# S1 in a tile of its own and first of seven products, S2·T2 fourth, and the first sigmoid ahead of the conversions

## The chip, the cores and the metric

The kernel runs on one core of a Trainium2 chip. A core has five engines with an instruction queue each: TensorE (PE in the profile, its weight loads PEld), VectorE (DVE), ScalarE (ACT), GpSimd (POOL, here almost only an issuer of DMAs) and SyncE (SP, an issuer of DMAs alone). The metric is the device time of one execution in microseconds (us). The kernel before took 982.21 us, the median of three runs (981.42 to 986.92).

## The reference

Softmaxes over q and k, a linear attention, and then a gated feed-forward layer, all in float32:

```python
q_s = exp(q - max(q, -1));  q_s = q_s / (sum(q_s, -1) + 1e-9)     # q, k, v: 8 x 8 x 576 x 64
k_s = exp(k - max(k, 2));   k_s = k_s / (sum(k_s, 2) + 1e-9)
kv  = einsum('bhsd,bhse->bhde', k_s, v)
x   = einsum('bhsd,bhde->bhse', q_s, kv)  ->  4608 tokens x 512
out = (sigmoid(x @ w_gate) * (x @ w_val)) @ w_out                 # d_ff = 1536
```

The weights come as float64.

## The kernel before, in words

**Tiles.** The 4608 tokens are cut into 9 token tiles of 512 (`w` = 0 to 8), the 1536 hidden columns into 12 blocks of 128 (`j`), or 6 pairs of blocks (`p`).

**First token tile** (w = 0, lines 1006 to 1043). For each `j`, `g1_0(j)` makes gate and value of one block in plain float32, two PSUM tiles of the pool `ps_gv` (three buffers, tile name `gv`); `g_sig_0` (ACT) and `g_mul_0` (DVE) make `h_0`; `g2_0(j-1)` multiplies with the block of w_out. Around them stands all one-time work, written out by hand in the order in which each engine's queue takes it:
- the float64 weights are narrowed to float32 (`w_low`, `w_top`, `w_join`, and `wo_low`, `wo_top`, `wo_join` for w_out), in passes that alternate between DVE and ACT;
- `split_hi` (ACT) and `split_lo` (DVE) split each pair's weights into a rounded part and a remainder, `wo_hi` and `wo_save` do so with w_out, and POOL's queue stores both to DRAM (`s_dram`, `wo_dram`);
- the side work of token tile 1: `k_max_send` and `k_max_read` send the maxima of k through DRAM on POOL's queue (for batches up to 2), and `qT_split(1, hp)` splits the q part that `x_mm(1, hp)` multiplies. It is called in `beside_first`, ahead of the step's conversions, and puts its DVE subtraction (line 514) right behind ACT's copy (line 513).

**Token tiles 1 to 8** (lines 1054 to 1078). 48 steps, one for each token tile and pair. `g1(w, p)` multiplies 2x2 blocks of weights and tokens in Winograd's way: seven products in place of eight, each of 12 matmuls with 256 moving columns (two halves, two row blocks, and three pairs of rounded part and remainder). The stationary operand is a block of weights: A11, A12 and A22 lie in the pair's own tile `a_w[p]`, the sums S1 to S4 in `s_sb`, which every step loads anew (`s_load`, line 278, POOL's queue: the sum for the next step, right behind this step's product). The moving operand is one of seven token blocks (`c_hl`: B11, T1, T2, B21, T3, B22, T4). They accumulate in three PSUM tiles `y`, `z` and `rr`, in the order A11 in y, S1 in z, S2 in y, A12 in rr, S3 in y, S4 in z, A22 in y. y and z are copied out by ACT between products (lines 673, 675, 678, 683), since each copy is a partial sum that the result needs: y after A11, after S2 and after S3. `h_split` makes the stationary operands of `g2`, the 24 matmuls of 512 columns (line 723) that follow one step later. `side_a` and `side_b` put the softmax of the next token tile beside them.

**What sets the order.** Nothing is reordered (`manual_schedule`): each engine works its queue front to back, as the code is written. A matmul that would write a PSUM tile waits until the copy ahead of it has read it. Weight loads run beside the matmul ahead of them.

**Addresses.** Two padding tiles shift pools against each other. Modulo 512 bytes all stationary operands of the split products (`s_sb`, `a_w`, `h`, `kv_sb`) begin at one place, all moving ones (`c_hl`, `wo_hl`, the ring that holds the split q) 320 bytes further on.

Of the kernel before, what the change touches and what calls it, by code (L numbers as in the profile page):

```python
# [8 lines left out]
F32 = mybir.dt.float32  # L9
F32R = mybir.dt.float32r  # L10
# [4 lines left out]
ALU = mybir.AluOpType  # L15
# [36 lines left out]
def attn_moe(ctx: ExitStack, tc: tile.TileContext, qf, qn, qT, k, kT, v, wg, wv, wo, out):  # L52
# [19 lines left out]
    ps_gv = ctx.enter_context(tc.tile_pool(name="ps_gv", bufs=3, space=bass.MemoryType.PSUM))  # L72
    ps_at = ctx.enter_context(tc.tile_pool(name="ps_at", bufs=1, space=bass.MemoryType.PSUM))

    s_sb = const.tile([P, 4, 2, 2, 2 * P], F32R, name="s_sb")
    x_32 = const.tile([P, NP, T], F32, name="x_32")
    sg = const.tile([P, 4, 2, HT], F32, name="sg")
    kv_sb = const.tile([P, 2, 2, NP, P], F32R, name="kv_sb")
# [173 lines left out]

    def split_of(p):
        f = f_w[p].rearrange("p b n e -> p b (n e)")
        s = s_sb.rearrange("p s h n e -> p s h (n e)")
        a = a_w[p].rearrange("p b h n e -> p b h (n e)")
        return [(a[:, A11:A12 + 1], f[:, 0:2])] + [
            (s[:, i:i + 1], t) for i, t in enumerate(s_32[p])
        ] + [(a[:, A22:A22 + 1], f[:, 3:4])]

    def split_hi(p):
# [5 lines left out]
    def split_lo(p):  # L267
        for o, x in split_of(p):
            nc.vector.tensor_tensor(  # L269
                out=o[:, :, 1], in0=x, in1=o[:, :, 0].bitcast(F32), op=ALU.subtract  # L270
            )
        nc.gpsimd.dma_start(
            out=s_dram[p], in_=s_sb.rearrange("p s h n e -> p (s h n e)").bitcast(F32)
        )

    def s_load(p, i):
        n = 4 * 2 * P
        nc.gpsimd.dma_start(  # L278
            out=s_sb[:, i].rearrange("p h n e -> p (h n e)"),
            in_=s_dram[p][:, i * n:(i + 1) * n].bitcast(F32R),  # L280
        )

# [227 lines left out]
    def qT_split(w, hp):  # L510
        t = qT_sb.pop((w, hp))
        hi, lo = (ring.tile([P, T], F32R, name="ring") for _ in range(2))
        nc.scalar.copy(out=hi, in_=t)
        nc.vector.tensor_tensor(out=lo, in0=t, in1=hi.bitcast(F32), op=ALU.subtract)
        qT_hl[w, hp] = (hi, lo)


    x_ps = {}
# [97 lines left out]
    def g_sig_0(j):  # L616
        h_0[j] = two.tile([P, T], F32, name="h_0", tag="h_lo")
        nc.scalar.activation(h_0[j], gate[j][0], AF.Sigmoid)  # L618
# [26 lines left out]
    def g1(w, p, s_next=None):  # L645

        y, z, rr = (ps_gv.tile([P, 2, HT], F32, name="gv") for _ in range(3))
        a, s = a_w[p], s_sb

        def prod(ps, ws, i, first, last):  # L650
            for n in range(2):
                wh, wl = ws(n)
                for kt in range(2):
                    for lh, x in ((wh, 0), (wh, 1), (wl, 0)):
                        nc.tensor.matmul(  # L655
                            ps[:, n], lhsT=lh(kt), rhs=c_hl[i][:, x, kt],
                            start=(first and n == 0 and kt == 0 and lh is wh and x == 0),
                            stop=(last and n == 1 and kt == 1 and lh is wl),
                            skip_group_check=True,
                        )  # L660

        def wa(i):
            return lambda n: [lambda kt, h=h: a[:, i, h, n, kt * P:(kt + 1) * P] for h in range(2)]

        def wsum(i):
            return lambda n: [lambda kt, h=h: s[:, i, h, n, kt * P:(kt + 1) * P] for h in range(2)]

        def more(i):
            if s_next is not None:
                s_load(s_next, i)  # L670

        prod(y, wa(A11), B11, True, False)
        nc.scalar.copy(out=sg[:, 0], in_=y)  # L673
        prod(z, wsum(S1), T1, True, False)
        nc.scalar.copy(out=sg[:, 2], in_=z)  # L675
        more(S1)
        prod(y, wsum(S2), T2, False, False)
        nc.scalar.copy(out=sg[:, 1], in_=y)  # L678
        more(S2)
        prod(rr, wa(A12), B21, True, True)  # L680
        nc.vector.tensor_tensor(out=sg[:, 0], in0=rr, in1=sg[:, 0], op=ALU.add)  # L681
        prod(y, wsum(S3), T3, False, False)
        nc.scalar.copy(out=sg[:, 3], in_=y)  # L683
        more(S3)
        nc.vector.tensor_tensor(out=sg[:, 3], in0=sg[:, 3], in1=sg[:, 2], op=ALU.add)  # L685
        prod(z, wsum(S4), B22, False, True)
        nc.vector.tensor_tensor(out=sg[:, 1], in0=z, in1=sg[:, 1], op=ALU.add)  # L687
        nc.scalar.activation(sg[:, 0:2, 0], sg[:, 0:2, 0], AF.Sigmoid)  # L688
        more(S4)
        prod(y, wa(A22), T4, False, True)  # L690
        nc.scalar.activation(sg[:, 3, 0], sg[:, 3, 0], AF.Sigmoid)
        nc.scalar.activation(sg[:, 2, 0], y[:, 0], AF.Sigmoid)
        tt = nc.vector.tensor_tensor
        tt(out=sg[:, 0:2, 0], in0=sg[:, 0:2, 0], in1=sg[:, 0:2, 1], op=ALU.mult)  # L694
        tt(out=sg[:, 3, 0], in0=sg[:, 3, 0], in1=sg[:, 3, 1], op=ALU.mult)
        tt(out=sg[:, 2, 0], in0=y[:, 1], in1=sg[:, 2, 0], op=ALU.mult)
# [122 lines left out]
    def beside_first(j):  # L819
        if j == 6:  # L820
            k_done(1)
        if 7 <= j <= 10:
            x_ev(1, j - 7)
        if 6 <= j <= 9:
            qT_split(1, j - 6)

    def after_first(j):
        if j == 0:
            for hp in range(NP):
                k_max(1, hp)  # L830
            k_max_send(1)
            k_max_read(1)
        if j == 1:
            for c in range(NC):
                qn_max(1, c)
        if j == 2:
            for c in range(NC):
                qn_sub(1, c)
        if j == 3:
            for c in range(NC):  # L840
                qn_exp(1, c)
            for hp in range(NP):
                k_sum(1, hp)
            for t in range(5):
                k_sub(1, t)
        if j == 4:
            for t in range(5):
                k_exp(1, t)
            for c in range(NC):
                qn_sum(1, c)  # L850
            for hp in range(NP):
                qf_mul(1, hp)
        if j == 5:
            for t in range(5):
                k_mm(1, t)
        if 6 <= j <= 9:
            x_mm(1, j - 6)
        if 5 <= j <= 8:
            qf_tr(1, j - 5, ps_gv.tile([P, T], F32, name="gv"))
        if j in (2, 5, 7, 9):  # L860
            load_next(1, {2: 1, 5: 2, 7: 3, 9: 4}[j])
        if j == 10:
            c_subs()
            load_next(1, 5, range(2))
            for i in (B11, T1, T2, B21):
                c_split(i)
        if j == 11:
            for t in range(2, 5):
                v_load(2, t)
# [135 lines left out]
    splits = {2: 0, 5: 1, 7: 2, 9: 3, 10: 4, 11: 5}  # L1005
    for j in range(NJ):
        g1_0(j)
        beside_first(j)
        split = splits.get(j)
        if split is not None:  # L1010
# [12 lines left out]
            w_low(j + 3)  # L1023
        if j + 2 < NJ:
            wo_low(j + 2)
        g_sig_0(j)
        if j > 0:
            wo_save(j - 1)
        if j + 3 < NJ:
            load_wo(j + 3)  # L1030
        if j + 5 < NJ - 1:
# [9 lines left out]
        if j == 3:  # L1041
            kv_split(0, lambda sl: kv_0[sl, :, sl])
        after_first(j)

    wo_hi(NJ - 1)
    g_mul_0(NJ - 1)
# [70 lines left out]
```

## Time and profile before

| | |
|---|---|
| median of three runs | 982.21 us |
| the profiled execution | 986.01 us |
| its span (first to last instruction) | 984.2 us |
| PE busy, of the span | 954.0 us, 97% |
| ACT, DVE, POOL busy | 471.4, 613.1, 167.3 us |
| mean granted TensorE clock | 0.985 |
| first product of the 48 steps begins | 181.67 us |
| DMA, mean over the span | 262 GB/s |

How to read the profile. The *groups* give for a line, an engine, an operation and its tiles the count, the busy time, the mean time of one, and the idle time of the engine just before, with what ended it. In the *timeline* a row is `start, length, engine, line, operation, tiles, shapes, count`, with the idle time before it and what ended it in brackets; rows of one kind that follow each other are merged. A matmul's length there is a latency: matmuls overlap, and the pace is the distance from start to start. *Waits* list who waited for whom: microseconds in total, times, the longest. The *chain* follows the last instruction back to what released each step.

### The profile page before, as it was taken

The page shows a single profiled execution, that of the slowest core. Times are in us where ns is not written, and L with a number is a line of the kernel's source. Part 1 is how long each engine was busy: PE and PEld are TensorE (multiplying, and loading weights), DVE is VectorE, ACT ScalarE, POOL GpSimd, SP SyncE. Part 2 cuts the span into 40 slices and gives each one's busy share as a digit, 9 for nine tenths or more (in the row PEclk, how much of TensorE's full clock was granted, in tenths as well). Part 3 has the DMA queues.
Part 4 walks back from the last instruction along what each step waited for, and adds up shares of the span by engine and source line. Part 5 has one row for each costly group of instructions (what it writes and reads, how often), then busy time and mean ns, then how long its engine had stood idle before and what let it go on. Part 6 is the DMA issues. An engine that isn't in the chain of part 4 may idle for free.

```text
span 984.2 us, 15634 instructions
## 1 busy us (share of the span) xinstructions
PE 954.0 (97%) x6062; PEld 824.0 (84%) x6062; DVE 613.1 (62%) x1013; ACT 471.4 (48%) x812; POOL 167.3 (17%) x316
## 2 busy tenths in 40 slices
PE   5899999799999999999999999999999999999998
PEld 5544544599999999999989999899999999999997
DVE  8688778776666566755684667557654655463242
ACT  4589785553436354525362545353434434533222
POOL 0110001221122112111111111121112121212210
PEclk7899999899999999999999999999999999999999
DMA  9987484899699978998899869996998779858662
GB/s 337 330 244 267 165 291 166 302 350 323 203 245 361 306 229 212 374 284 259 180 381 304 261 143 375 332 276 132 374 317 239 216 237 312 248 176 251 199 206 74
DMA packets 93864, 257.78 MB, mean 262 GB/s; under 512 B 15264, under 2 KB 17568, under 8 KB 93024
## 3 DMA queue, kind: packets, MB, share of 16 engines
q0 software_dynamic: 43712, 168.32, 56.9%
q1 hardware_dynamic: 50080, 88.48, 30.6%
q8 instruction: 48, 0.79, 0.4%
q14 instruction: 24, 0.20, 0.1%
HBM read 228.20 MB, written 28.56 MB: 261 GB/s over the span
## 4 chain that ended last, share of the span: by engine, by line
PE 66%; DMA 17%; DVE 7%; ACT 7%; issue 2%; SPq 1%; POOL 0%; DVEq 0%; ACTq 0%; POOLq 0%
PE gv L655 37%; PE acc L723 19%; DMA ring<-k_in 3%; DMA q_m_row<-q_m 3%; PE gv L610 3%; DMA q_b<-q_m_row 3%; DMA kmax_row<-k_max 2%; PE gv L538 2%; DMA ring<-qT_in 1%; PE at L378 1%; PE acc L637 1%; DMA ring<-qn_in 1%; DMA s<-s_sb 1%; DMA wo<-wo_hl 1%; PE at L538 1%
## 5 line engine op out<-in xcount | busy, mean ns | idle before, releaser
L655 PE MATMUL gv<-c_hl,s_sb 128*128 128x256 f32 x2304 | 288.1, 280 | 4.3 <-ACT sg L673 4.2
L655 PEld LDWEIGHTS gv<-c_hl,s_sb 128*128 128x128 f32 x2304 | 276.7, 188 | 6.9 <-ACT sg L673 6.5
L723 PE MATMUL acc<-wo_hl,h 128*128 128x512 f32 x1152 | 272.2, 392 | 0.0
L723 PEld LDWEIGHTS acc<-wo_hl,h 128*128 128x128 f32 x1152 | 213.1, 188 | 44.3
L655 PE MATMUL gv<-c_hl,a_w 128*128 128x256 f32 x1728 | 226.1, 279 | 0.7 <-DVE a_w L269 0.7
L655 PEld LDWEIGHTS gv<-c_hl,a_w 128*128 128x128 f32 x1728 | 214.9, 188 | 5.2 <-issue 1.0
L278 POOL DMA_DIRECT2D s_sb<-s x188 | 100.1, 532 | 321.8 <-PE gv L655 317.5
L681 DVE TENSOR_TENSOR sg<-gv,sg 128x512 f32<-128x512 f32 x48 | 33.2, 691 | 163.0 <-PE gv L655 163.0
L234 POOL DMA_DIRECT2D wo_hl<-wo x96 | 50.9, 531 | 297.6 <-PE acc L723 295.4
L683 ACT COPY sg<-gv 128x512 f32<-128x512 f32 x48 | 28.1, 586 | 106.4 <-PE gv L655 106.4
L610 PE MATMUL gv<-x,f_w 128*128 128x512 f32 x160 | 72.4, 606 | 5.5 <-ACT h L618 5.5
L673 ACT COPY sg<-gv 128x512 f32<-128x512 f32 x48 | 28.0, 583 | 89.8 <-PE gv L655 65.1
L685 DVE TENSOR_TENSOR sg<-sg 128x512 f32<-128x512 f32 x48 | 33.2, 692 | 58.9 <-ACT sg L683 58.9
L610 PEld LDWEIGHTS gv<-x,f_w 128*128 128x128 f32 x160 | 30.5, 194 | 43.7 <-issue 36.0
L706 DVE TENSOR_TENSOR h<-sg,h 128x1024 fp32r<-128x1024 f32 x48 | 58.8, 1226 | 1.6
L688 ACT ACTIVATE sg<-sg 128x512 f32<-128x512 f32 x48 | 30.3, 632 | 55.8 <-DVE sg L687 55.8
L694 DVE TENSOR_TENSOR sg<-sg 128x512 f32<-128x512 f32 x48 | 33.2, 693 | 33.5 <-ACT sg L688 33.5
L637 PE MATMUL acc<-wo_t,h 128*128 128x512 f32 x96 | 45.3, 617 | 5.7 <-DVE h L622 5.6
L678 ACT COPY sg<-gv 128x512 f32<-128x512 f32 x48 | 28.1, 586 | 44.7 <-PE gv L655 44.7
L637 PEld LDWEIGHTS acc<-wo_t,h 128*128 128x128 f32 x96 | 18.8, 199 | 30.0 <-issue 21.7
L675 ACT COPY sg<-gv 128x512 f32<-128x512 f32 x48 | 28.1, 586 | 26.2 <-PE gv L655 26.1
L412 ACT CAST kv_sb<-kmax_b 64x256 fp32r<-64x256 f32 x14 | 5.7, 404 | 67.1 <-DVE kmax_b L388 66.8
(152 smaller groups left out, 1054.8 us busy)
## 6 DMA issues: line engine op xcount, KB each, us to landing
s_sb<-s POOLq DMA_DIRECT2D x188, 512.0 KB, 7.6
wo_hl<-wo POOLq DMA_DIRECT2D x96, 512.0 KB, 6.0
s<-s_sb POOLq DMA_DIRECT2D x6, 2048.0 KB, 7.6
out<-x SPq DMA_DIRECT2D x36, 256.0 KB, 9.6
ring<-k_in SPq DMA_DIRECT2D x28, 256.0 KB, 15.0
ring<-qn_in SPq DMA_DIRECT2D x28, 256.0 KB, 10.3
q_b<-q_m_row SPq DMA_DIRECT2D x56, 128.0 KB, 8.6
ring<-qT_in SPq DMA_DIRECT2D x28, 256.0 KB, 8.9
```

What stands on the lines that cost most here:

```text
L234: nc.gpsimd.dma_start(out=t.rearrange("p h e -> p (h e)"), in_=wo_dram[2 * p + i].bitcast(F32R))
L278: nc.gpsimd.dma_start(out=s_sb[:, i].rearrange("p h n e -> p (h n e)"), in_=s_dram[p][:, i * n:(i + 1) * n].bitcast(F32R),)
L538: nc.tensor.matmul(ps[:, f:t], lhsT=kl if lh else kh, rhs=rh[:, f:t], start=(lh == 0 and rh is qh), stop=(lh == 1),)
L610: nc.tensor.matmul(ps[n], lhsT=w[:, kt // 2, sl], rhs=x_0[:, kt], start=(kt == 0), stop=(kt == NK - 1),)
L637: nc.tensor.matmul(acc[0][m], lhsT=h_0[j][:, m * P:(m + 1) * P], rhs=wo_t[j // 2][:, j % 2], start=(j == 0), stop=(j == NJ - 1),)
L655: nc.tensor.matmul(ps[:, n], lhsT=lh(kt), rhs=c_hl[i][:, x, kt], start=(first and n == 0 and kt == 0 and lh is wh and x == 0), stop=(last ...
L681: nc.vector.tensor_tensor(out=sg[:, 0], in0=rr, in1=sg[:, 0], op=ALU.add)
L685: nc.vector.tensor_tensor(out=sg[:, 3], in0=sg[:, 3], in1=sg[:, 2], op=ALU.add)
L688: nc.scalar.activation(sg[:, 0:2, 0], sg[:, 0:2, 0], AF.Sigmoid)
L694: tt(out=sg[:, 0:2, 0], in0=sg[:, 0:2, 0], in1=sg[:, 0:2, 1], op=ALU.mult)
L706: nc.vector.tensor_tensor(out=lo, in0=sg[:, :, 0], in1=hi.bitcast(F32), op=ALU.subtract)
L723: nc.tensor.matmul(acc[w][m], lhsT=h[lh][:, i, sl], rhs=o[i][:, rh], start=(at == 0 and i == 0 and lh == 0 and rh == 0), stop=(at == NS - ...
```

## The change

Four edits. (1) `s_sb` is cut into `s_234` (S2 to S4) and `s_1` (S1), with padding tiles of 80 and 48 words around `s_1`. S1's stationary operand then begins where the moving ones do, modulo 512 bytes; S2 to S4 and everything else stay where they were. The two padding tiles make 512 bytes together. The store of the sums becomes two DMAs. (2) In `g1` S1·T1 comes first, and S2·T2 behind A12·B21 in place of ahead of it. (3) In the first token tile the sigmoid of block 0 comes ahead of the conversions of that step. (4) `qT_split(1, hp)` leaves its DVE subtraction to `qT_low`, called just ahead of `x_mm(1, hp)`, and `wo_save(j-1)` moves behind `after_first(j)`.

```diff
-    s_sb = const.tile([P, 4, 2, 2, 2 * P], F32R, name="s_sb")
+    s_234 = const.tile([P, 3, 2, 2, 2 * P], F32R, name="s_234")
+    const.tile([P, 80], F32, name="pad_s")
+    s_1 = const.tile([P, 1, 2, 2, 2 * P], F32R, name="s_1")
+    const.tile([P, 48], F32, name="pad_x")
+    def s_at(i):
+        return s_1[:, 0] if i == S1 else s_234[:, i - S2]
...
-        nc.gpsimd.dma_start(
-            out=s_dram[p], in_=s_sb.rearrange("p s h n e -> p (s h n e)").bitcast(F32)
-        )
+        n = 4 * 2 * P
+        for t, i0, i1 in ((s_1, 0, 1), (s_234, 1, 4)):
+            nc.gpsimd.dma_start(
+                out=s_dram[p][:, i0 * n:i1 * n],
+                in_=t.rearrange("p s h n e -> p (s h n e)").bitcast(F32),
+            )
...
         hi, lo = (ring.tile([P, T], F32R, name="ring") for _ in range(2))
         nc.scalar.copy(out=hi, in_=t)
+        qT_hl[w, hp] = (hi, lo)
+        if w >= NF:
+            qT_low(w, hp, t)
+        else:
+            qT_sb[w, hp] = t
+
+    def qT_low(w, hp, t):
+        hi, lo = qT_hl[w, hp]
         nc.vector.tensor_tensor(out=lo, in0=t, in1=hi.bitcast(F32), op=ALU.subtract)
-        qT_hl[w, hp] = (hi, lo)
...
-        prod(y, wa(A11), B11, True, False)
-        nc.scalar.copy(out=sg[:, 0], in_=y)
         prod(z, wsum(S1), T1, True, False)
         nc.scalar.copy(out=sg[:, 2], in_=z)
         more(S1)
+        prod(y, wa(A11), B11, True, False)
+        nc.scalar.copy(out=sg[:, 0], in_=y)
+        prod(rr, wa(A12), B21, True, True)
+        nc.vector.tensor_tensor(out=sg[:, 0], in0=rr, in1=sg[:, 0], op=ALU.add)
         prod(y, wsum(S2), T2, False, False)
         nc.scalar.copy(out=sg[:, 1], in_=y)
         more(S2)
-        prod(rr, wa(A12), B21, True, True)
-        nc.vector.tensor_tensor(out=sg[:, 0], in0=rr, in1=sg[:, 0], op=ALU.add)
         prod(y, wsum(S3), T3, False, False)
...
         if 6 <= j <= 9:
+            qT_low(1, j - 6, qT_sb.pop((1, j - 6)))
             x_mm(1, j - 6)
...
         g1_0(j)
+        if j == 0:
+            g_sig_0(j)
         beside_first(j)
...
-        g_sig_0(j)
         if j > 0:
-            wo_save(j - 1)
+            g_sig_0(j)
...
         after_first(j)
+        if j > 0:
+            wo_save(j - 1)
```

**PE, the seven products of one step** (token tile 1, its sixth step), before. `gv_1975` is y, `gv_1976` z and `gv_1977` rr; behind the arrow stand the token block and the weights:

```order
L655 MATMUL gv_1975<-c_hl_1052,a_w_987 128x256 x12
L655 MATMUL gv_1976<-c_hl_1052,s_sb_100 128x256 x12
L655 MATMUL gv_1975<-c_hl_1057,s_sb_100 128x256 x12
L655 MATMUL gv_1977<-c_hl_1057,a_w_987 128x256 x12
L655 MATMUL gv_1975<-c_hl_1104,s_sb_100 128x256 x12
L655 MATMUL gv_1976<-c_hl_1104,s_sb_100 128x256 x12
L655 MATMUL gv_1975<-c_hl_1109,a_w_987 128x256 x12
```

The same step of the changed kernel, where `gv_1984` is y, `gv_1985` z, `gv_1986` rr, and line 673 is what was line 655:

```order
L673 MATMUL gv_1985<-c_hl_1058,s_1_102 128x256 x12
L673 MATMUL gv_1984<-c_hl_1058,a_w_994 128x256 x12
L673 MATMUL gv_1986<-c_hl_1063,a_w_994 128x256 x12
L673 MATMUL gv_1984<-c_hl_1063,s_234_100 128x256 x12
L673 MATMUL gv_1984<-c_hl_1113,s_234_100 128x256 x12
L673 MATMUL gv_1985<-c_hl_1113,s_234_100 128x256 x12
L673 MATMUL gv_1984<-c_hl_1118,a_w_994 128x256 x12
```

Before, no two neighbours write the same PSUM tile. Now the fourth and the fifth (S2 and S3) both write y. With the semaphores that each waits for, the third to the fifth product of the changed kernel read:

```order
L673 MATMUL gv_1986<-c_hl_1063,a_w_994 128x256 [waits Activation_49]
L673 MATMUL gv_1986<-c_hl_1063,a_w_994 128x256 x11
L673 MATMUL gv_1984<-c_hl_1063,s_234_100 128x256 [waits DMASW7_49,Activation_49]
L673 MATMUL gv_1984<-c_hl_1063,s_234_100 128x256 x11
L673 MATMUL gv_1984<-c_hl_1113,s_234_100 128x256 [waits DMASW0_49,Activation_49]
L673 MATMUL gv_1984<-c_hl_1113,s_234_100 128x256 x11
```

The count that the first matmul of the fifth product waits for on ACT's semaphore is that of the copy of y behind the fourth (line 698 of the changed kernel, line 678 before).

**DVE, step j = 9 of the first token tile**, before, from its first row on. `ring<-gv,ring` is the remainder of the split q, `wo_hl` that of w_out (`wo_save`), `a_w` the first row of `split_lo`:

```order
L514 TENSOR_TENSOR ring<-gv,ring 128x512
L169 SCALAR_TENSOR_TENSOR f_last<-f_last,sg 128x2x256 x2
L169 SCALAR_TENSOR_TENSOR wo_t<-wo_t,wo_raw 128x512
L622 TENSOR_TENSOR h_873<-gv,h_873 128x512
L140 TENSOR_SCALAR wo_raw<-wo_raw 128x512
L153 SCALAR_TENSOR_TENSOR wo_raw<-wo_raw 128x512
L222 TENSOR_TENSOR wo_hl<-wo_t,wo_hl 128x512
L269 TENSOR_TENSOR a_w<-f_w,a_w 128x2x512
```

The end of that step in the changed kernel, from the last row of `w_sums(4)` on:

```order
L254 TENSOR_TENSOR s_957<-f_w,s_955 128x512
L533 TENSOR_TENSOR ring<-gv,ring 128x512
L317 TENSOR_REDUCE k_max<-kt_109 128x1
L318 TENSOR_SCALAR k_neg<-k_max 128x1
L317 TENSOR_REDUCE k_max<-kt_110 128x1
L318 TENSOR_SCALAR k_neg<-k_max 128x1
L230 TENSOR_TENSOR wo_hl<-wo_t,wo_hl 128x512
```

The remainder of the split q has gone from the step's first row to a place behind `split_lo` and `w_sums`, and that of w_out from ahead of `split_lo` to behind the maxima of k.

More of the change, by code (lines that the diff above doesn't have):

```diff
@@ L254, in split_of @@
         f = f_w[p].rearrange("p b n e -> p b (n e)")
-        s = s_sb.rearrange("p s h n e -> p s h (n e)")
+        s = [s_at(i).rearrange("p h n e -> p h (n e)").unsqueeze(1) for i in range(4)]
         a = a_w[p].rearrange("p b h n e -> p b h (n e)")
         return [(a[:, A11:A12 + 1], f[:, 0:2])] + [
-            (s[:, i:i + 1], t) for i, t in enumerate(s_32[p])
+            (s[i], t) for i, t in enumerate(s_32[p])
         ] + [(a[:, A22:A22 + 1], f[:, 3:4])]
@@ L278, in s_load @@
         nc.gpsimd.dma_start(
-            out=s_sb[:, i].rearrange("p h n e -> p (h n e)"),
+            out=s_at(i).rearrange("p h n e -> p (h n e)"),
             in_=s_dram[p][:, i * n:(i + 1) * n].bitcast(F32R),
@@ L647, in g1 @@
         y, z, rr = (ps_gv.tile([P, 2, HT], F32, name="gv") for _ in range(3))
-        a, s = a_w[p], s_sb
+        a = a_w[p]
         def prod(ps, ws, i, first, last):
@@ L665, in wsum @@
         def wsum(i):
-            return lambda n: [lambda kt, h=h: s[:, i, h, n, kt * P:(kt + 1) * P] for h in range(2)]
+            return lambda n: [lambda kt, h=h: s_at(i)[:, h, n, kt * P:(kt + 1) * P] for h in range(2)]
         def more(i):
```

## The prediction

> **What bounds the kernel now.** I read the page first: busy time, the chain that ended last, the costliest groups.
>
> ```profile
> PE 954.0 (97%) x6062; PEld 824.0 (84%) x6062; DVE 613.1 (62%) x1013; ACT 471.4 (48%) x812; POOL 167.3 (17%) x316
> PE 66%; DMA 17%; DVE 7%; ACT 7%; issue 2%; SPq 1%; POOL 0%; DVEq 0%; ACTq 0%; POOLq 0%
> L655 PE MATMUL gv<-c_hl,s_sb 128*128 128x256 f32 x2304 | 288.1, 280 | 4.3 <-ACT sg L673 4.2
> L723 PE MATMUL acc<-wo_hl,h 128*128 128x512 f32 x1152 | 272.2, 392 | 0.0
> L655 PE MATMUL gv<-c_hl,a_w 128*128 128x256 f32 x1728 | 226.1, 279 | 0.7 <-DVE a_w L269 0.7
> ```
>
> PE is busy for 97% of the span, and its three costliest groups, the products of the 48 steps and the second multiplication, make 786 of 954 us with hardly any idle time ahead of them. Next I asked who waits in the 48 steps.
>
> ```profile
> PEld gv L655 <- ACT sg L673: 6.5, 11, 0.8
> ```
>
> From 206 us on this is the only wait of PE's weight loads that the view lists, and its matmuls wait for nothing else either: 6.5 us in 11 places, all for the copy of y behind A11. No wait for a DMA appears. So a stall of PE that is added in the steps is added to the time in full, and only these 6.5 us are there to be won back. PE's other waits lie in the first token tile.
>
> **The new wait behind S2.** S2 and S3 now follow each other on y, and S3's first matmul waits for ACT's copy of S2's result. Before, a product on another tile stood between. The timeline has each piece of the new wait, in two steps that lie beside each other:
>
> ```profile
> 301.21 1.52 PE L655 MATMUL gv<-c_hl,a_w 128*128 128x256 f32 x12
> 301.41 0.58 ACT L678 COPY sg<-gv 128x512 f32<-128x512 f32 x1 [0.77 <-PE gv L655]
> ...
> 312.14 1.52 PE L655 MATMUL gv<-c_hl,a_w 128*128 128x256 f32 x12
> ...
> 313.50 1.52 PE L655 MATMUL gv<-c_hl,s_sb 128*128 128x256 f32 x12
> ...
> 314.97 0.56 ACT L673 COPY sg<-gv 128x512 f32<-128x512 f32 x1
> ...
> 315.58 1.68 PE L655 MATMUL gv<-c_hl,s_sb 128*128 128x256 f32 x12 [0.55 <-ACT sg L673]
> ...
> 317.10 1.57 PE L655 MATMUL gv<-c_hl,a_w 128*128 128x256 f32 x12
> ```
>
> ```profile
> L678 ACT COPY sg<-gv x48: 585/587/589, 187.5 to 963.9; 128x512 f32<-128x512 f32 x48
> ```
>
> The copy at 301.41 starts 0.20 us behind the first matmul of the next product (301.21), thus some 0.31 behind the last matmul of its own, one pace of 0.11 earlier. It takes 0.587 (585 to 589 ns in all 48 steps). At 315.53 (314.97 + 0.56) a copy ends for which PE waits, and PE goes on at 315.58, 0.05 later. Unhindered, the next matmul would have come after 0.12. The product that starts out of a wait takes 1.52 from its start to the next one (315.58 to 317.10) where the following ones of that step take 1.41 (1.57 is that plus the last one's latency, as 1.52 is to 1.36 at 312.14): 0.11 more. Together 0.31 + 0.587 + 0.05 - 0.12 + 0.11 = 0.94 us, in each of 48 steps: **+45.1 us**. ACT stands idle ahead of that copy (0.77 us at 301.41), so it can't come earlier; were it late, the wait would be longer. Behind the waiting matmul stand S3, S4, A22 and the 24 matmuls of line 723, and behind these the whole rest: nothing on PE can go around it.
>
> **The old wait goes.** S2 now comes two products behind the start of A11, as before, but S1's copy and A11's have one product more until ACT must have caught up with its backlog. In the step above, S2 starts 2.08 us behind S1 (313.50 to 315.58) in place of 1.36. In the new order S2 would be due at 312.14 + 3 x 1.36 = 316.22; ACT, free at 314.97, has done two copies of 0.587 by 316.14, in time. With the 0.11 behind each of 11 waits, the 6.5 us make 7.7; some 0.1 may stay in two or three steps: **-7.5 us**, between -4 and -8.
>
> The reload of S1 (`s_sb<-s`, issued behind its product) stays a whole step ahead of its use, and that of S2, one product later, is needed one product later.
>
> **S1's own rate, and the two paces.** Steps without any wait differ:
>
> ```profile
> 348.70 1.52 PE L655 MATMUL gv<-c_hl,a_w 128*128 128x256 f32 x12
> ...
> 358.22 5.66 PE L723 MATMUL acc<-wo_hl,h 128*128 128x512 f32 x24
> ...
> 397.74 1.57 PE L655 MATMUL gv<-c_hl,a_w 128*128 128x256 f32 x12
> ...
> 407.63 2.68 PE L723 MATMUL acc<-wo_hl,h 128*128 128x512 f32 x11
> ```
>
> The same 84 matmuls take 9.52 us in one and 9.89 in the other, 113.3 and 117.7 ns each, with the same addresses modulo 512. Counted by these distances, 9 of 48 steps run at the fast pace throughout; the first and the last:
>
> ```profile
> 232.76 1.52 PE L655 MATMUL gv<-c_hl,a_w 128*128 128x256 f32 x12
> ...
> 242.28 1.99 PE L723 MATMUL acc<-wo_hl,h 128*128 128x512 f32 x8
> ```
>
> ```profile
> 753.00 1.52 PE L655 MATMUL gv<-c_hl,a_w 128*128 128x256 f32 x12
> ...
> 762.52 1.76 PE L723 MATMUL acc<-wo_hl,h 128*128 128x512 f32 x7
> ```
>
> So the pace depends on how a step is entered, not on addresses alone. Were all steps fast, the other 39 would give up to 39 x 0.37 = 14 us (13, as some are fast in part). Were all slow, it would cost 3 to 4. After a wait the step above went on slowly (1.41 a product behind 315.58, 1.36 ahead of it), which costs the three products behind the new wait little, since most are slow already: **+1 us**.
>
> What S1's 576 matmuls take with both operands at one remainder, no split product shows. The nearest rows:
>
> ```profile
> 322.75 1.95 PE L378 MATMUL at<-v,ring 128*128 128x128 f32 x16
> ...
> 324.53 3.04 PE L378 MATMUL at<-f_last,ring 128*128 128x128 f32 x24
> ```
>
> ```profile
> 666.37 2.69 PE L538 MATMUL gv<-ring,kv_sb 128*128 128x384 f32 x18
> 668.89 1.03 PE L538 MATMUL at<-ring,kv_sb 128*128 128x384 f32 x6
> ```
>
> ```profile
> 32.50 3.17 PE L561 MATMUL acc<-q,f_last 128*128 128x512 f32 x7
> ...
> 35.51 10.46 PE L610 MATMUL gv<-x,f_w 128*128 128x512 f32 x24
> ```
>
> From below: matmuls with half the columns still take 111 ns (1.78 us for 16), so a pace under 111 is not to be had: 576 x (111 - 117) = -3.5 us. From above: the products of line 538 take 140 ns for 256 columns on average (2.52 us for 18): 576 x 23 = +13. In plain float32 line 561, whose operands do share a remainder, takes 0.43 us a pass (3.01 for 7), and line 610, whose don't, takes the same. I take **0**, by this last and nearest pair, and keep both ends. [...]
>
> **The clock.** A wait of PE can cost clock besides:
>
> ```profile
> 104.00:109.00 5.00, 3.67 (x5) 1.61 (x6) 4.56 (x12) 4.53 (x7) 0.00 (x0) 0.66 0.99 419
> ...
> 312.00:316.00 4.00, 3.45 (x29) 3.21 (x28) 2.94 (x7) 4.00 (x9) 1.07 (x2) 1.00 1.11 405
> ```
>
> In the window with the wait of 0.55 us the granted clock stays at 1.00, while around the 2.01 us of waiting ahead of 105.33 (quoted below) it is 0.66. The new 0.84 us is near the first; I take 0. [...]
>
> **The first token tile.** At its start the sigmoid goes ahead:
>
> ```profile
> 49.41 3.70 PE L610 MATMUL gv<-x,f_w 128*128 128x512 f32 x8 [3.44 <-ACT h L618]
> ...
> 69.18 0.62 ACT L218 CAST wo_hl<-wo_t 128x512 fp32r<-128x512 f32 x1 [4.05 <-DMA wo<-wo_hl]
> ```
>
> ```profile
> 105.33 8.83 PE L610 MATMUL gv<-x,f_w 128*128 128x512 f32 x16 [2.01 <-ACT h L618]
> ```
>
> PE's 3.44 us at 49.41 go, but PE waits for ACT again at 105.33, and ACT's work up to there hangs on the DMA that landed at 69.18, which the edit doesn't touch. I cost it at **0**: the 3.44 us turn up as a longer wait at 105.33. At the end of the tile it is otherwise:
>
> ```profile
> 143.23 0.69 DVE L514 TENSOR_TENSOR ring<-gv,ring 128x512 fp32r<-128x512 f32 x1 [2.79 <-ACT ring L513]
> ```
>
> ```profile
> 156.71 0.76 POOL L319 DMA_DIRECT2D kmax_row<-k_max  x1 [4.22 <-DVE k_neg L307]
> 167.65 0.55 POOL L323 DMA_DIRECT2D kmax_b<-kmax_row  x1 [10.17 <-DMA kmax_row<-k_max]
> ```
>
> ```profile
> 178.05 2.17 ACT L265 CAST s_sb<-s 128x512 fp32r<-128x512 f32 x4 [4.26 <-DMA s<-s_sb]
> ```
>
> ```profile
> 176.55 5.68 PE L637 MATMUL acc<-wo_t,h 128*128 128x512 f32 x8 [5.61 <-DVE h L622]
> ```
>
> The last of these waits is PE's 5.61 us; ACT's at 178.05 hands on to the first product at 181.67. Both end a chain: maxima of k on DVE, sent at 156.71, read at 167.65, and only then the stores of POOL's queue, whose landing frees the sums at 178.05. DVE's 2.79 us of idling at 143.23 lie ahead of the maxima and go; `wo_save`, as large as the row at 143.23 (0.69), moves behind them. So the chain starts 2.79 + 0.69 = 3.5 us earlier: **-3.5 us**, between 0 (if a DMA then lands no earlier) and -5.6 (PE's wait). What is late next is ACT's `split_hi`. The six stores more cost POOL 0.55 us each in idle time; `wo_save` is past `split_lo`'s stores on POOL, and its buffers are wanted again only two steps on.
>
> **The sum**, against the profiled execution's 986.0 us: 986.0 + 45.1 - 7.5 + 1 + 0 - 3.5 + 0 = 1021.1 us, 35.1 more. The profiled execution is 3.8 us above the median of 982.2, which I put down to the paces, so the forecast for the median is **1017.3 us**.
>
> **Rivals.**
> - *All steps fast* (S1 at the front sets the pace). For it: the pace is set at a step's entry. Against: the new wait comes behind it and may set it anew. 13 + 1 us less: 1003.
> - *S1 itself slow.* Up to +13: 1030. Only the rows of line 538 speak for it.
> - *The change doesn't stall*: the copy is hidden. Without the 45.1: 972. Against it stands the order, with S3 behind S2 on one tile and its wait.
> - *The pace itself falls* to 107 ns by S1's new place and order: 4032 x (117 - 107) = 40 us less, 977, faster than before. It decides from 117 - 34/4032 = 109 ns on; below that the kernel is faster. Against it: 111 ns for half the columns.
> - *The clock halves* for some 3.4 us behind each new wait, as around 105.33: 48 x 1.7 = 82 us more, 1099. Against it: 1.00 at 312.
>
> **Chances.** Forecast 0.63, all fast 0.15, S1 slow 0.15, clock 0.03, no stall 0.02, lower pace 0.02. The forecast's own range is 1011 to 1024 (the bounds of the old wait and the first tile); with the first two rivals, 1003 to 1030, and outside stay 0.07 and the far ends. Faster by over 0.5% (about 5 us, what a measurement can tell from no change) comes from the two small cases: 0.04. Within 0.5%: 0.01. Slower: 0.95.
>
> **What would show it.** Right: PE's L673 waits for ACT's L698 48 times, some 0.8 us each by the matmuls' idle time; A11's copy (L694) no longer ends a wait; the first product begins near 178. Wrong: no such wait, or a pace of S1's product far from 113 to 118 ns (12 of them 1.36 to 1.41 us), or products behind the wait that are all fast, or a first product later than 181.67.

## The result: 4% slower, and the profile after

| | before | changed | ratio, 95% interval |
|---|---|---|---|
| runs beside the prediction | 981.82 us (4 runs) | 1021.94 us (2 runs) | 1.0399 [1.0331, 1.0468] |
| repeated, label e1_after | 983.66 us (23 runs) | 1020.04 us (4 runs) | 1.0357 [1.0325, 1.0390] |

The ratios lie near those of the mean times (1021.94 to 982.69 in the first row), not of the medians.

In two other runs of the changed kernel, the profiled one among them, TensorE ran at under a fifth of its pace (5474 us; in the profiled one 679 ns on the mean from matmul to matmul in the products, where e1_after has some 117); they are left out, and the profile shown here is that of e1_after, which is the same kernel (1020.5 us, span 1018.4).

From its page, the engines' busy time and the groups that answer to those of before:

```profile
PE 963.3 (95%) x6062; PEld 826.3 (81%) x6062; DVE 612.8 (60%) x1013; ACT 471.1 (46%) x812; POOL 170.5 (17%) x322
...
L673 PE MATMUL gv<-c_hl,s 128*128 128x256 f32 x2304 | 300.4, 282 | 32.4 <-ACT sg L698 32.4
...
L741 PE MATMUL acc<-wo_hl,h 128*128 128x512 f32 x1152 | 272.6, 392 | 0.0
...
L673 PE MATMUL gv<-c_hl,a_w 128*128 128x256 f32 x1728 | 216.7, 278 | 2.6 <-ACT h L636 2.6
```

PE's work is hardly more than before, but ahead of the products with the sums now stand 32.4 us of idle time, where there were 4.3. The waits of PE and of its weight loads in the steps:

```profile
PEld gv L673 <- ACT sg L698: 42.0, 48, 0.9
...
PE gv L673 <- ACT sg L698: 32.4, 48, 0.7
```

48 waits, one a step, all for ACT's copy of y behind S2. Who waited for the copy behind A11 (line 694), which was PE's only wait in the steps before:

```profile
who waited for it (us, times):
  DVE sg L696: 32.0, 8
  POOL wo L233: 2.7, 1
```

PE is not in that list any more. One step in the timeline (PE, and ACT's copy behind S2):

```profile
334.89 1.60 PE L673 MATMUL gv<-c_hl,s 128*128 128x256 f32 x12
336.33 2.99 PE L673 MATMUL gv<-c_hl,a_w 128*128 128x256 f32 x24
339.16 1.57 PE L673 MATMUL gv<-c_hl,s 128*128 128x256 f32 x12
341.41 3.09 PE L673 MATMUL gv<-c_hl,s 128*128 128x256 f32 x24 [0.68 <-ACT sg L698]
344.34 1.57 PE L673 MATMUL gv<-c_hl,a_w 128*128 128x256 f32 x12
...
340.77 0.58 ACT L698 COPY sg<-gv 128x512 f32<-128x512 f32 x1 [2.24 <-PE gv L673]
```

S2 takes 2.25 us from its start to S3's (339.16 to 341.41) in place of 1.41, and S3 and S4 together 2.93 in place of 2.82: 0.84 + 0.11 = 0.95 us. The copy begins 0.31 behind S2's last matmul (340.46, one pace ahead of 340.57), lasts 0.58, and PE goes on 0.06 behind its end.

To put sums to this, the distances from start to start of all matmuls are taken from the trace, from the third step's first matmul to the program's last (46 steps). A distance of over 205 ns within the products counts as a wait, less 116 ns:

| third step to the end | before | changed |
|---|---|---|
| third step begins | 211.78 us | 207.65 us |
| from there to the last matmul | 768.36 us | 805.96 us |
| waits and the slow matmul behind each | 8.0 us | 43.4 us |
| mean of the other distances in the products | 116.66 ns | 117.13 ns |
| mean distance in line 723 / 741 | 229.72 ns | 229.97 ns |

Of the 37.6 us that the 46 steps lost, 35.4 are waits; the other 2 are pace (0.47 ns on 3726 matmuls are 1.75 us, 0.25 ns on 1082 are 0.27).

### The profile page after: what moved, and what is told of

Its sections match the earlier page's. It is cut to its first block, busy times and chain, and to the rows that moved or that the text cites. A ratio compares the mean times of both kernels' runs of the same rounds, so it can differ in the third digit from the quotient of the medians.

```text
span 5472.1 us, 15649 instructions
## 1 busy us (share of the span) xinstructions
PE 5430.4 (99%) x6062; PEld 4374.7 (80%) x6062; DVE 617.2 (11%) x1013; ACT 478.4 (9%) x812; POOL 169.9 (3%) x322
## 4 chain that ended last, share of the span: by engine, by line
PE 99%; ACT 1%; issue 0%; DVE 0%; POOL 0%; POOLq 0%
PE gv L673 49%; PE acc L741 28%; PE gv L628 9%; PE acc L655 5%; PE at L389 3%; PE gv L556 2%; PE at L556 1%; PE gv L944 1%; ACT sg L698 1%; PE acc L376 0%; PE acc L579 0%; PE gv L511 0%; PE acc L969 0%; PE acc L955 0%; PE at L511 0%
## 5 line engine op out<-in xcount | busy, mean ns | idle before, releaser
L673 PEld LDWEIGHTS gv<-c_hl,s 128*128 128x128 f32 x2304 | 1556.8, 939 | 109.4 <-ACT sg L698 69.0
L673 PE MATMUL gv<-c_hl,s 128*128 128x256 f32 x2304 | 1593.0, 1036 | 32.4 <-ACT sg L698 32.4
L741 PE MATMUL acc<-wo_hl,h 128*128 128x512 f32 x1152 | 1541.5, 1694 | 0.0
L741 PEld LDWEIGHTS acc<-wo_hl,h 128*128 128x128 f32 x1152 | 1033.4, 909 | 436.5 <-issue 421.1
L673 PE MATMUL gv<-c_hl,a_w 128*128 128x256 f32 x1728 | 1179.7, 1034 | 0.0
L673 PEld LDWEIGHTS gv<-c_hl,a_w 128*128 128x128 f32 x1728 | 1172.5, 948 | 0.0
L628 PE MATMUL gv<-x,f_w 128*128 128x512 f32 x160 | 426.3, 3020 | 0.0
L628 PEld LDWEIGHTS gv<-x,f_w 128*128 128x128 f32 x160 | 144.7, 910 | 264.0 <-issue 262.1
L655 PE MATMUL acc<-wo_t,h 128*128 128x512 f32 x96 | 258.4, 3035 | 0.0
L389 PE MATMUL at<-f_last,ring 128*128 128x128 f32 (+1 forms) x160 | 111.7, 1052 | 0.0
```

What stands on the lines that cost most here:

```text
L389: nc.tensor.matmul(kvps[b][:, hp], lhsT=kt[:n, sl], rhs=vt[:n, sl], start=(t == 0 and hp == 0), stop=(t == len(KTILES) - 1 and hp == NP - ...
L628: nc.tensor.matmul(ps[n], lhsT=w[:, kt // 2, sl], rhs=x_0[:, kt], start=(kt == 0), stop=(kt == NK - 1),)
L655: nc.tensor.matmul(acc[0][m], lhsT=h_0[j][:, m * P:(m + 1) * P], rhs=wo_t[j // 2][:, j % 2], start=(j == 0), stop=(j == NJ - 1),)
L673: nc.tensor.matmul(ps[:, n], lhsT=lh(kt), rhs=c_hl[i][:, x, kt], start=(first and n == 0 and kt == 0 and lh is wh and x == 0), stop=(last ...
L741: nc.tensor.matmul(acc[w][m], lhsT=h[lh][:, i, sl], rhs=o[i][:, rh], start=(at == 0 and i == 0 and lh == 0 and rh == 0), stop=(at == NS - ...
```

## Experiments

All ratios are against the kernel before, timed beside each group on the same chip: e1 to e4 (median of before 983.66 us), e5 to e8 (980.54) and e9 to e12 (986.99). Times of different groups are compared by their ratios. "Third step" and the sums are read as in the table above.

**e1_after**, the changed kernel again.

> The changed kernel again, for a profile that can be laid beside that of before. Theory: some 40 us slower than before; PE's line 673 waits for ACT's line 698 48 times with 0.8 to 0.9 us each, about 40 us in all, and 45 us with the slower first product behind the wait; A11's copy (line 694) ends no wait; the first product of the steps begins near 178 us; S1's product takes 1.36 to 1.41 us like the others. Rival 'S1 itself slow': S1's 12 matmuls take more than 1.45 us. Rival 'paces': the waits make less than the gap, and the rest comes from more steps at 117.7 ns a matmul (before: 9 of 48 steps at 113.3 throughout).

1020.04 us, 1.0357 [1.0325, 1.0390]. 48 waits as shown. S1's product takes 1.42 to 1.44 us in 43 of the 48 steps and not 1.36 to 1.41; the first product begins earlier than foretold, and the wait has moved into the step:

```profile
173.66 1.99 PE L673 MATMUL gv<-c_hl,s 128*128 128x256 f32 x12
178.28 3.09 PE L673 MATMUL gv<-c_hl,a_w 128*128 128x256 f32 x24 [2.64 <-ACT h L636]
...
207.65 1.60 PE L673 MATMUL gv<-c_hl,s 128*128 128x256 f32 x12
```

S1 starts at 173.66, and A11 then waits 2.64 us for ACT. So the start of a product isn't what the first token tile is to be measured by; the third step's is.

**e2_order_alone**: the kernel before with the order alone.

```diff
-        prod(y, wa(A11), B11, True, False)
-        nc.scalar.copy(out=sg[:, 0], in_=y)
         prod(z, wsum(S1), T1, True, False)
...
-        prod(y, wsum(S2), T2, False, False)
...
+        prod(y, wa(A11), B11, True, False)
+        nc.scalar.copy(out=sg[:, 0], in_=y)
         prod(rr, wa(A12), B21, True, True)
...
+        prod(y, wsum(S2), T2, False, False)
```

> Only the order of the seven products is changed, the sums stay in one tile and the first token tile stays as before. Theory: the order carries all of the loss, so +36 to +42 us against before (45 for the wait behind S2, 7.5 less for the wait behind A11, 1 for the pace), 1018 to 1024 us, and the first product at 181.67 us as before. Rival 'S1 slow by its place in memory': this kernel is quicker than the changed one by up to 13 us in spite of the old first token tile.

1026.53 us (4 runs), 1.0436 [1.0404, 1.0468]: 42.9 us more than before, all of the loss and somewhat more than the 36 to 42 foretold. In the trace the waits are those of the changed kernel (43.46 us), but every step is slow: the other distances have a mean of 117.84 ns against 117.13, which makes 2.6 us, and the third step begins at 210.66, 3.0 later. So S1's new place and the first token tile take some 6 to 8 us off what the order costs.

**e3_tile_alone**: S1's own tile, with the old order and the old first token tile.

```diff
-    s_sb = const.tile([P, 4, 2, 2, 2 * P], F32R, name="s_sb")
+    s_234 = const.tile([P, 3, 2, 2, 2 * P], F32R, name="s_234")
+    const.tile([P, 80], F32, name="pad_s")
+    s_1 = const.tile([P, 1, 2, 2, 2 * P], F32R, name="s_1")
+    const.tile([P, 48], F32, name="pad_x")
```

> Only S1's tile is moved, with the old order and the old first token tile; three more DMA stores than before are issued per two pairs, nothing else. Theory: within 3 us of before (0 for the address, 0 for the stores); S1's product at 1.36 to 1.41 us. Rival 'S1 slow': up to +13 us, and S1's 12 matmuls take over 1.45 us. Rival 'lower pace': S1's product under 1.33 us and up to 3.5 us less.

980.61 us (12 runs), 0.9967 [0.9952, 0.9982]. A fast step of it, where S1 and S2 are the 24 matmuls at 295.32:

```profile
293.96 1.52 PE L666 MATMUL gv<-c_hl,a_w 128*128 128x256 f32 x12
295.32 2.96 PE L666 MATMUL gv<-c_hl,s 128*128 128x256 f32 x24
298.12 1.52 PE L666 MATMUL gv<-c_hl,a_w 128*128 128x256 f32 x12
299.48 2.88 PE L666 MATMUL gv<-c_hl,s 128*128 128x256 f32 x24
```

They take 2.80 us (1.44 and 1.36, where 1.36 to 1.41 was expected of S1), S3 and S4 at 299.48 take 2.72. Single distances in S1 are 120 ns, whether 113 or 118 stand ahead of it. The steps together took 768.22 us in this profile, as before (768.36); where the 3 us of the timed runs come from, this trace doesn't show.

**e4_head_alone**: the first token tile alone (edits 3 and 4).

```diff
+        if j == 0:
+            g_sig_0(j)
         beside_first(j)
...
-        g_sig_0(j)
         if j > 0:
-            wo_save(j - 1)
+            g_sig_0(j)
...
         after_first(j)
+        if j > 0:
+            wo_save(j - 1)
```

`qT_low` stands ahead of `x_mm` as in the change.

> Only the first token tile is changed: the first sigmoid ahead of the conversions, the subtraction of q's split just ahead of its product, and the saving of w_out behind the side work; the old tile of the sums and the old order. Theory: -3.5 us (0 to -5.6) against before, first product of the steps near 178 us in place of 181.67, and PE's wait of 3.44 us at 49 us gone but turned up as a longer wait near 105 us. Rival 'both edits are worth nothing': the first product stays at 181 to 182 us and the time within 1 us.

981.50 us (12 runs), 0.9975 [0.9953, 0.9997]; third step at 206.50 (211.78 in the first profile of before, 210.54 in the second, e9). The first product begins at 171.57 us, not near 178. The timeline, from ACT's copy of the split (line 513) to the sending of the maxima:

```profile
140.37 0.59 ACT L513 CAST ring<-gv 128x512 fp32r<-128x512 f32 x1
...
141.94 1.23 DVE L269 TENSOR_TENSOR a_w<-f_w,a_w 128x1024 fp32r<-128x1024 f32 x1 [2.59 <-ACT a_w L265]
...
151.33 0.77 POOL L319 DMA_DIRECT2D kmax_row<-k_max  x1 [4.82 <-DVE k_neg L307]
```

From the copy's end (140.96) to the sending it is 10.37 us; before, from the end of DVE's wait for it, 13.48 (143.23 to 156.71). That is 3.1 us less. DVE still idles 2.59 us, now for ACT's cast of the weights, but its conversions, which followed the subtraction, are done by then.

**e10_sigmoid_alone**: edit 3 alone.

```diff
+        if j == 0:
+            g_sig_0(j)
         beside_first(j)
...
-        g_sig_0(j)
         if j > 0:
+            g_sig_0(j)
             wo_save(j - 1)
```

> Only the first sigmoid ahead of the conversions, everything else as before. Theory: nothing (within 1 us): PE's 3.44 us near 49 us shrink but turn up near 105 us, since ACT's chain up to there hangs on a DMA; the maxima of k are sent as in the kernel before of the same call. Rival 'the sigmoid carries the gain of the first token tile': -2 us, as with all of that tile's edits.

988.07 us (10 runs) beside 986.99, 1.0005 [0.9981, 1.0029]; maxima sent at 154.97, beside 155.14 in e9.

```profile
141.49 0.69 DVE L514 TENSOR_TENSOR ring<-gv,ring 128x512 fp32r<-128x512 f32 x1 [2.81 <-ACT ring L513]
...
154.97 0.76 POOL L319 DMA_DIRECT2D kmax_row<-k_max  x1 [4.23 <-DVE k_neg L307]
```

From the end of DVE's wait to the sending it is 13.48 us, as before, so the 3.1 us of e4 are edit 4's. The sigmoid shows no gain; the interval would still hide 1.9 us of it. Edit 4 was not run alone.

**e5_tile_head**: all of the change but the order.

> The changed kernel with the old order of products: S1's own tile and the new first token tile stay. Theory: no wait behind S2, so all of the loss goes and what the tile (-3.0 us when alone) and the first token tile (-2.2 alone) bring stays; both bring the first products forward through the same chain (third step at 208.35 and at 206.50 us against 211.78 before), so they don't add up in full: 977 to 980 us against some 983.5 before. Rival 'they add up': 975 to 977. S1's product takes 1.43 to 1.44 us as with the tile alone, and more steps than before are fast.

976.92 us (11 runs) beside 980.54, 0.9962 [0.9946, 0.9978], third step at 203.47. Without the order there is no wait behind S2 (in the steps behind the first, PE's weight loads wait for the copy behind A11 alone, 5.7 us in 8 places), and the other edits are a small gain: by the ratio 3.7 us, against 3.2 (e3) and 2.5 (e4) apart. The intervals are too wide to say whether the two add up.

**e6_between_six** and **e7_between_three**: the changed kernel, with 6 (or 3) of the 24 matmuls of `g2` of the step before between S2 and S3.

```diff
         prod(y, wsum(S2), T2, False, False)
         nc.scalar.copy(out=sg[:, 1], in_=y)
         more(S2)
+        if beside is not None:
+            g2_part(*beside, 0, 6)
         prod(y, wsum(S3), T3, False, False)
```

> The changed kernel with its order of products, but 6 of the 24 matmuls of 512 columns of the step before stand between S2 and S3 (and 18 behind A22 as before). Theory: S3 has to begin 0.95 us behind S2's last matmul; the six take 1.37, so PE has work while ACT copies, and the wait is gone in 47 of 48 steps: 44 us less than the changed kernel, about 975 us, and up to 13 less if, with no wait left, the steps stay at the pace of 113 ns. PE's line 673 waits for the copy behind S2 once (in the first step). Rival 'the loss is in the new order itself or in S1's place (paces, memory)': it stays above 1000 us.

> As the one with six, but with three matmuls of 512 columns (0.69 us) between S2 and S3. Theory: 0.95 - 0.12 - 0.69 = 0.15 us of waiting is left in each of 47 steps, and 0.11 behind each wait if that does not depend on its length: 12 us in all, so about 988 us, 32 less than the changed kernel, with all products behind S2 slow. Rival 'any work between is enough': as with six, about 975.

Six: 980.83 us (12 runs), 0.9996 [0.9976, 1.0016]. Three: 988.57 (7 runs), 1.0059 [1.0035, 1.0084]. PE's weight loads wait in the steps from 200 us on, with six:

```profile
PEld gv L673 <- ACT sg L694: 10.2, 13, 1.1
```

and with three:

```profile
PEld gv L673 <- ACT sg L698: 19.2, 46, 0.4
PEld gv L673 <- ACT sg L694: 3.0, 7, 0.5
```

With work for PE during the copy, the wait behind S2 is gone with six and small with three (988.57 is the 988 foretold, 3.0 us of other waits included). The 19.2 us are idle time of the weight loads, much of it beside the three matmuls: from the start of the third of them to that of S3 it is 0.38 us (median), where with six matmuls it is 0.23, so 0.15 us a step are lost, as foretold. With six it should have been 975: the wait for the copy behind A11, which the change had removed, is back, with 11.2 us in all. One possible reason is that taking six matmuls out of the row ahead of S1 brings A11 1.37 us nearer to ACT's backlog; this was not tested.

**e8_s4_third**: the changed kernel with S4 between S2 and S3, so that S3 and A22 meet on y.

```diff
-        prod(y, wsum(S3), T3, False, False)
...
         prod(z, wsum(S4), B22, False, True)
...
+        prod(y, wsum(S3), T3, False, False)
```

> The changed kernel with S4 between S2 and S3: z stands between S2 and S3, but S3 and A22 are now neighbours on y. Theory: with S1 first, four products on y have only two others between them, so the wait only moves: PE waits 48 times for the copy behind S3 (0.84 us and 0.11 behind it), and the time is that of the changed kernel within 4 us, 1016 to 1024. Rival 'what costs is the place of S2 behind A12': about 975 us.

1015.73 us (4 runs), 1.0356 [1.0324, 1.0387], the ratio of the changed kernel. The waits of the changed kernel turn up behind S3's copy:

```profile
PEld gv L673 <- ACT sg L704: 42.0, 48, 0.9
...
PE gv L673 <- ACT sg L704: 32.4, 48, 0.7
```

In both pairs tried (S2 and S3, S3 and A22) the price belongs to two neighbours on one tile.

**e9_before_again**: the kernel before, profiled a second time.

> The kernel before once more, for a second profile of it. It tells how much of the first profiled execution was its own. The prediction put the 3.8 us between that execution (986.0) and the median down to the two paces. If so, the maxima of k are sent at 156.7 us and the third step begins at 211.8 us again, and the share of fast steps differs. Rival: the first profiled execution was late in its first token tile (the kernel with only the order changed, whose first token tile is the same code, sent the maxima at 152.8): then the sending is at 151 to 154 us here, the third step begins some 3 to 4 us earlier than 211.8, and the matmuls of the steps take 116 to 117 ns as before.

985.35 us when profiled, on a chip where the kernel before has a median of 986.99.

```profile
141.67 0.69 DVE L514 TENSOR_TENSOR ring<-gv,ring 128x512 fp32r<-128x512 f32 x1 [2.79 <-ACT ring L513]
...
155.14 0.77 POOL L319 DMA_DIRECT2D kmax_row<-k_max  x1 [4.23 <-DVE k_neg L307]
```

```profile
PEld gv L655 <- ACT sg L673: 10.6, 16, 1.6
```

The maxima go out at 155.14 against 156.71, and at 152.82 in e2, 152.73 in e3, 154.07 in e11, which all share this code (but for e3's store in two parts): the first token tile varies by 4 us between executions, while 13.47 us from DVE's wait to the sending are the same. So neither expectation of this run is met as it stands: the maxima go out later than the rival's 151 to 154 us, and the third step begins at 210.54, 1.2 us earlier and not 3 to 4. The steps are another mix: 18 of 48 are fast throughout in place of 9, and the mean distance is 115.61 ns in place of 116.66, 4 us less; but the waits for ACT grew from 8.0 to 12.8 us, and from the third step to the end it is 768.94 us against 768.36.

**e11_sums_moved**: the kernel before with all four sums where the moving operands begin modulo 512.

```diff
+    const.tile([P, 80], F32, name="pad_s")
     s_sb = const.tile([P, 4, 2, 2, 2 * P], F32R, name="s_sb")
+    const.tile([P, 48], F32, name="pad_x")
```

> The kernel before with all four sums (one tile, as before) at the place modulo 512 where the moving operands begin; order and first token tile as before. S1 alone there took 1.43 to 1.44 us in place of 1.36 or 1.41. Theory 'a price of the shared remainder': all four products take 1.43 to 1.44, that is +0.02 to +0.08 us each or up to 192 x 0.05 = 10 us more, less what more fast steps bring (up to 13): 978 to 992 us. Rival 'the price is that of changing from one place to another': only the first product of a group (S1, and S3 behind A12) is above 1.42, and the others are at 1.36 or 1.41.

990.29 us (10 runs), 1.0031 [1.0006, 1.0057]. A step without a wait:

```profile
246.85 1.52 PE L657 MATMUL gv<-c_hl,a_w 128*128 128x256 f32 x12
248.21 3.04 PE L657 MATMUL gv<-c_hl,s_sb 128*128 128x256 f32 x24
251.09 1.52 PE L657 MATMUL gv<-c_hl,a_w 128*128 128x256 f32 x12
252.45 3.04 PE L657 MATMUL gv<-c_hl,s_sb 128*128 128x256 f32 x24
255.33 1.52 PE L657 MATMUL gv<-c_hl,a_w 128*128 128x256 f32 x12
```

Each pair of sums takes 2.88 us, 1.44 a product, the second of a pair too; A11 and A12 take 1.36 here, as A22 does in all 48 steps. So it is a price of the shared place (120 ns a matmul), not of the change from one place to another. Only these two places, 320 bytes apart, were tried.

**e12_read_later**: e5 with the reading back of the maxima behind the stores of the sums on POOL's queue.

```diff
                 k_max_send(b)
-                k_max_read(b)
+                if n > 1:
+                    k_max_read(b)
...
             split_lo(split)
+            if split == 4:
+                k_max_read(2)
```

> The old order with S1's tile and the new first token tile, and besides this the reading back of the maxima of k (for the third batch) is issued behind the two stores of the fifth pair's sums instead of ahead of them on POOL's queue. Theory: the chain ahead of the first product was sending, 9 us of waiting for its landing, reading, and only then the stores; the stores now go out at about 157 us in place of 161.2, the first step's waits (1.2 to 4.5 us a product) shrink, and the third step begins 3 to 4.5 us earlier: 3 to 4 us less than the kernel without this, 973 to 974 us if that is at 977. Rival 'other work is as late': nothing changes, within 1 us.

980.52 us (10 runs) beside 986.99, 0.9924 [0.9891, 0.9956]. The stores go out 4.6 and 3.4 us earlier than in e5 (whose second is at about 161.8), but ACT's casts that wait for their landing don't. Here:

```profile
156.60 0.53 POOL L282 DMA_DIRECT2D s<-s  x1 [3.54 <-DVE s L277]
158.41 0.53 POOL L282 DMA_DIRECT2D s<-s  x1 [1.27 <-DVE s L277]
...
172.45 1.66 ACT L273 CAST s<-s 128x512 fp32r<-128x512 f32 x3 [4.60 <-DMA s<-s]
```

and in e5:

```profile
161.20 1.14 POOL L282 DMA_DIRECT2D s<-s  x2
...
171.40 1.66 ACT L273 CAST s<-s 128x512 fp32r<-128x512 f32 x3 [4.10 <-DMA s<-s]
```

Landing takes 14.0 us behind the second issue in place of some 9.6, and the third step begins at 204.18 against 203.47. But the e12 execution was late already ahead of the maxima, at ACT's copy of the split. In e12:

```profile
140.80 0.59 ACT L524 CAST ring<-gv 128x512 fp32r<-128x512 f32 x1
```

and in e5:

```profile
138.92 0.59 ACT L524 CAST ring<-gv 128x512 fp32r<-128x512 f32 x1
```

Counted from there, the stores go out 6.5 and 5.3 us earlier than in e5, the casts begin only 0.8 earlier and the third step 1.2. So by these two profiles most of the theory falls: the read ahead of them held the stores' issue, but not what ends the chain. The ratio is the best of all kernels here and 3.7 us below that of e5, which would be the 3 to 4 foretold, yet the intervals overlap, and the profile shows a third of that at most.

## Why the prediction held, step by step

Its time was 1017.3 us, 1.0357 times the 982.21; measured were 1.0357 and 1.0399, so it fell 3 to 5 us short in the two medians, within the range of 1011 to 1024. That one ratio agrees to the last digit is luck: the terms below are off by up to 1.3 us each, in both directions. The lower end of the range doesn't follow from the two bounds named for it, which give 1014.7; 1011.2 needs the -3.5 of S1's rate as well.

- **The new wait**, +45.1: right, with each of its pieces. Measured are 43.4 us in 46 steps, 0.943 a step, 45.3 in 48. e2 shows that the order alone brings it, e6 and e7 that it is the time of the copy (1.37 us of other work hide it, 0.69 leave a rest), and e8 that it goes with the adjacency. By the matmuls' idle time a wait is 0.68 us (32.4 / 48), not the 0.8 named as its sign; from start to start it is the 0.84 of the step above. The rival without a stall is out.
- **The old wait**, -7.5: right in size (8.0 us went, and PE waits for line 694 no more). The reason given, that S2 comes late enough by itself, isn't shown: in e6, where PE doesn't stall behind S2, it is back. That fits ACT catching up during the new wait, 0.84 us in every step, but e6 also moves six matmuls, so the two are not separated.
- **S1's own rate**, 0: the mis-sized term. With both operands at one remainder a matmul takes 120 ns (e3, e11): 1.42 to 1.44 us a product where 1.36 or 1.41 stand otherwise, some +1 us in 48 steps. I had taken the plain float32 rows as the nearest, and the split products differ from them; the bounds held. The other side of it was missed: behind S1 in its new place half of the steps run fast up to S2's wait, as here in the changed kernel:

```profile
351.27 1.58 PE L673 MATMUL gv<-c_hl,s 128*128 128x256 f32 x12
...
352.69 2.88 PE L673 MATMUL gv<-c_hl,a_w 128*128 128x256 f32 x24
...
355.41 1.52 PE L673 MATMUL gv<-c_hl,s 128*128 128x256 f32 x12
```

A11 and A12 take 2.72 us there and 2.83 in the step at 334.89. Against e2, where no step does this, it is 2.6 us less.

- **The pace**, +1: measured +2.0 with S1's place, and by e2 +4.4 without it (117.84 against 116.66 ns on 3726 matmuls): behind the new wait the products are slow (A22 takes 1.41 to 1.42 us, 118 ns a matmul: from 344.34 to 345.76 in the changed kernel, from 293.69 to 295.11 in e2).
- **The clock**, 0: right; from 178 to 1014 us of the changed kernel (e1_after), over all 48 new waits, the granted clock is 1.00, and the mean of the span is 0.991 against 0.985. The reason given, that 0.84 us is nearer to 0.55 than to 2.01, was not enough by itself: length alone doesn't decide (last section).
- **The first token tile**, -3.5: 3.1 by the chain up to the sending (e4), 2.2 by the medians; the sigmoid is 0 within its interval, as costed (e10). That its gain near 49 us (a wait there of 1.32 us in place of 3.44) turns up again near 105 isn't shown: the wait there is 1.98 us in e10, but with the old code 0.98 (e9), 2.01 (before) and none (e2). What was named to show it was wrong: the first product begins at 173.66 and not near 178, since a shorter wait there only moves into the step.
- **The 3.8 us** between the profiled execution and the median were put down to the paces. That isn't borne out: in e9 a pace that saves 4 us goes with 4.8 us more of waits, and the first token tile alone varies by 4 us.
- **All steps fast**, the rival at 1003: it didn't come: behind the new wait the products are slow also in the step at 351.27, where A11 and A12 take 2.72 us and A22 then 1.41 (360.54 to 361.95). Its price of 13 us may have been too high as well: in e9 more fast steps went with longer waits for ACT. Two executions don't show that the one caused the other.
- **S1 slow**: out; S1's product takes 1.42 to 1.44 us and not over 1.45. Even four such products in each step (e11) are 1.0031, about 3 us, with the other three products mostly at 1.36.

What stays open: what makes a step fast or slow beyond S1's place and a wait; why the tile alone is 0.3% faster in timed runs; what lands late in e12; and what decides, besides a wait's length, whether the clock drops.

## What to carry to other kernels

Where products accumulate in a few PSUM tiles and each partial sum is copied out, count for each tile its products and the others that can stand between them: if there are too few, moving one product to the front moves the wait (here from 11 places to all 48 steps), and its price can be added up from the copy's start, its length and the restart in a trace of before. Fill such a gap with other matmuls that are ready, and look where their leaving brings the next wait. Measure a change early in the program by the start of something behind the waits, and profile the kernel before twice, since single executions differ by as much as small edits bring.

## What the runs showed of the hardware

**Three paces.** The same matmul of 256 columns with its weight load takes 113.3, 117.7 or 120 ns from start to start: 120 where the sums were moved by 320 bytes, so that stationary and moving operand begin at one place modulo 512 (24 in 2.88 us in e11, 12 in 1.44 in e3), the others in steps of before with equal addresses (84 in 9.52 us from 348.70, in 9.89 from 397.74). Other places were not tried, so that 512 is the modulus that counts isn't shown.

**The clock behind a wait.** A window of the changed kernel with its wait, then e3 around a wait of 1.60 us and e12 around one of 2.04 (the column behind POOL's is the granted clock):

```profile
356.00:360.00 4.00, 3.33 (x29) 3.13 (x28) 0.42 (x2) 1.25 (x3) 0.84 (x2) 1.00 0.75 240
```

```profile
434.00:437.00 3.00, 2.01 (x17) 2.01 (x18) 2.49 (x6) 1.69 (x4) 0.33 (x1) 1.00 1.22 269
...
434.99 1.21 PE L666 MATMUL gv<-c_hl,s 128*128 128x256 f32 x8 [1.60 <-ACT sg L684]
```

```profile
332.00:334.00 2.00, 2.00 (x14) 2.00 (x13) 0.52 (x2) 0.59 (x1) 0.53 (x1) 0.60 1.27 270
...
330.93 1.75 PE L673 MATMUL gv<-c_hl,s 128*128 128x256 f32 x12 [2.04 <-ACT sg L691]
```

Behind 1.60 us it stays at 1.00, behind 2.04 it falls to 0.60. The wait near 105 us falls on the same sides: 0.98, 1.26 and 1.55 us (e9, e11, e4) leave it at 1.00 from 104 to 109 us, 1.62, 1.98 and 2.01 (the changed kernel, e10, before) are followed by 0.66, 0.68 and 0.66. In the profile before, the five windows of 1 us from 105 to 110 have 0.74, 0.50, 0.50, 0.55 and 1.00: 1.7 us lost, or 3.4 us at half the clock, as the prediction's rival has it. But a wait's length alone doesn't decide. The one near 49 us is 3.44 us long in the profile before and 3.46 in e9. Before:

```profile
49.40:53.40 4.00, 3.99 (x10) 1.84 (x11) 3.96 (x7) 4.00 (x5) 0.00 (x0) 1.00 0.47 16
```

and e9:

```profile
49.18 1.37 PE L610 MATMUL gv<-x,f_w 128*128 128x512 f32 x2 [3.46 <-ACT h L618]
...
49.20:53.20 4.00, 4.00 (x6) 1.78 (x7) 3.96 (x7) 4.00 (x5) 0.00 (x0) 0.59 0.49 16
```

The clock behind this wait is 1.00 in one execution and 0.59 in the other. The 2.64 us ahead of 178.28 in the changed kernel are followed by 1.00 as well:

```profile
178.00:182.00 4.00, 3.72 (x29) 3.57 (x30) 4.00 (x8) 3.27 (x7) 0.95 (x2) 1.00 1.06 428
```

So in the windows shown here no wait of up to 1.60 us is followed by a lower clock, and longer ones sometimes are: 1.62 us of idling, as the profile counts it, by 0.66 in one place, and 3.44 by 1.00 in another. By these numbers a wait of 1.62 us, 2.4 times the 0.68 of the new one, could have cost clock besides.
